# Projections in 64-row halves: the matmuls of q, k, v and the output as pairs in two phases, in a new order

## The chip, the cores and the metric

The kernel runs on one core of a Trainium2 chip. What counts is the time of one launch on the device, in microseconds (us): 454.13, the median of three runs from 454.07 to 455.19. The engines are TensorE (PE in the rows; PEld is its loading of weights), VectorE (DVE), ScalarE (ACT), GpSimd (POOL) and SyncE (SP), whose queue issues all the DMAs.

## What is computed

Eight batches of 8 heads, 576 positions, head size 64. Two attentions are added, and a mixture of four causal attention experts, two of which are chosen for each position, follows. Cut to the core:

```
out_up    = repeat(softmax(q_d @ k_d.T / 8) @ v_d, 4)        # q_d, k_d, v_d: means of 4 positions
out_local = softmax(where(|i-j| < 4, q @ k.T / 8, -1e9)) @ v
x         = (out_up + out_local) as [8, 576, 512]
logits    = x @ w_gate                                       # two of four experts, softmax over the two
for e in range(4):
    a    = softmax(causal((x @ wq[e]) @ (x @ wk[e]).T / 8))
    out += weight_of(e) * (a @ (x @ wv[e]) @ wo[e])
```

## The kernel before

Stage 1 of a batch works on four pairs of heads: local scores (`s1_local`, tile `sc`, line L515), pooled scores (`s1_down`, tile `scd`, L588), their transposes (`tp`, L383) and their products with v (`s1_out`, tile `o`, L650 to L662), from which x comes (L670). x is split into a rounded part `xh` (L675) and a rest `xl` (L676), so that a product with a weight, which is split too, is three matmuls at the rate of rounded fp32: `xh` with the high and the low part of the weight, and `xl` with the high part.

Stage 2 makes the projections. `project` (L686) makes q or k of two experts, 128 rows by 576 columns in a two-bank PSUM tile `pj`: twelve matmuls of 128 rows on 320 columns and twelve on 256 (four pairs of heads times three, L693). `project_by_pair` (L708) is the same for the first q, in the order in which the x arrive. `s2_v` makes v and the gate's logits for 128 positions at a time (12 matmuls on 260 columns, L739, two position blocks in one PSUM tile `pv`), and for the last 64 positions (8 matmuls, L748).

Stage 3 makes the causal scores (`sq`, L852), their softmax (DVE L872, ACT L875, and L883 on POOL or DVE), the transposes of its rows (`tq`, L383), the products with v (tile `o`, L966 and L970) and the output projection (`po`, L989: six matmuls on 256 and six on 320 columns; L1011 for the last batch).

So TensorE works in three shapes, which the rows show as rows * columns of the weights: 128*128 (`pj`, `pv`, `po`), 64*128 (the transposes `tp` and `tq`, in twos on the upper and the lower 64 rows) and 64*64 (`sc`, `scd`, `sq`, `o`, four at a time in the quarters of the array).

All PSUM use goes through four tiles of two banks (`big`). The order in which every step is issued is a table of numbers, `SEQ`, an entry for each step with the engine that does it; -1 is a filler matmul on zeros (`wu`, L472) that keeps TensorE busy. Work of stage 1 of a batch, stage 2 of the one before and stage 3 of the one before that stands mixed in it. A step's `alloc` names the tiles that it takes over and whose earlier readers it waits for.

Of the kernel before, what the change touches and what calls it, by code (L numbers as in the profile page):

```python
# [29 lines left out]
    968, 1092, 1040, 1044, 892, 1168, 100, 112, 104, 1332, 1336, 836, 1233, 1049, 972, 980, 1508, 828, 824, 820,  # L30
    1069, 1212, 1216, 1220, 1052, 1340, 1056, 1224, 1228, 976, 1152, 1156, 728, 732, 1172, 1008, 1012, 1513, 984,
    988, 1436, 934, 1098, 1160, 992, 1108, 1112, 1100, 1104, 1245, 1248, 1548, 1552, 1556, 1560, 1252, 1256, 1261,
    1432, 1753, 1564, 1004, 1460, 1464, 1568, 1572, 1468, 1756, 1576, 1264, 1268, 1580, 1164, 1272, 1277, 1292,
    1344, 1180, 1520, 1524, 1116, 1120, 1124, 1496, 1472, 1476, 1528, 1532, 1348, 1352, 1128, 1132, 1136, 1480,
    1537, 1540, 1356, 1544, 1484, 1488, 1384, 1284, 1500, 1296, 1288, 1300, 1176, 1184, 1360, 1364, 1368, 1592,
    1388, 1504, 1584, 1144, 1492, 1588, 1648, 1644, 2073, 1241, 1141, 1596, 1608, 1612, 1600, 1604, 1304, 1308,
    1312, 1316, 1616, 1392, 1396, 1765, 1768, 1320, 1716, 1328, 1324, 1620, 1624, 1720, 1728, 1016, 1020, 1400,
    1404, 1408, 2077, 1773, 1776, 1724, 1780, 1784, 1672, 1676, 1412, 1416, 1516, 1790, 1372, 1376, 1820, 2128,
    1680, 1732, 1736, 1740, 1744, 1420, 1424, 1280, 1429, 117, 1380, 1824, 2132, 1828, 1832, 2016, 1708, 1629, 1792,
    1712, 1796, 2085, 1664, 1668, 1444, 2328, 1188, 1192, 1836, 1685, 1688, 1448, 1440, 1652, 1660, 1988, 1656,  # L40
    1992, 2324, 2020, 2088, 1840, 1844, 2092, 1692, 2024, 1848, 2096, 1696, 1700, 1749, 2100, 1852, 2532, 2536,
    2028, 2032, 1760, 1996, 2004, 2000, 2409, 1856, 2116, 2248, 2252, 2413, 2104, 2540, 1632, 1636, 1640, 1704,
    2080, 2120, 2124, 2036, 2040, 2044, 2048, 1861, 1864, 1916, 1921, 1800, 1804, 1808, 2940, 1812, 1868, 1880,
    1884, 1872, 1876, 1924, 1936, 2352, 2356, 1928, 1932, 1888, 1944, 1892, 1948, 1940, 1904, 1908, 1912, 1897,
    1972, 1976, 109, 1901, 2108, 2944, 2464, 2360, 1980, 1984, 2472, 2476, 1953, 1956, 1816, 1968, 1960, 1965, 2365,
    2368, 2468, 2876, 2880, 2884, 2052, 2056, 2372, 2888, 2060, 2064, 2377, 2380, 2384, 2288, 2300, 2304, 2168,
    2180, 2172, 1452, 1456, 2136, 2140, 2144, 2332, 2292, 2184, 2176, 2296, 2212, 2340, 2848, 2336, 2984, 2980,
    2008, 2012, 2852, 2068, 2948, 2992, 2996, 2988, 2148, 2152, 2892, 2156, 2188, 2192, 2200, 2196, 2224, 2216,
    2421, 2424, 2428, 2432, 2165, 2896, 2436, 2440, 2308, 2900, 2160, 2572, 2576, 2580, 2228, 2220, 2284, 2396,
    2400, 2404, 2600, 2604, 2204, 2208, 2444, 2608, 2312, 2316, 3433, 2544, 2548, 2232, 2236, 2240, 2612, 2552,  # L50
    2556, 3008, 3012, 2320, 3016, 3020, 2480, 2484, 2488, 2492, 2496, 2904, 2500, 2508, 2417, 2344, 2348, 2864,
    2505, 2616, 2620, 2664, 2668, 2672, 2256, 2456, 2260, 2624, 2628, 2460, 2448, 2452, 2632, 2244, 2388, 2856,
    2392, 3436, 2908, 2636, 2644, 2640, 2560, 2564, 2708, 2720, 2724, 2728, 2264, 2268, 2712, 2768, 2780, 2784,
    2772, 2776, 2272, 2276, 2280, 2732, 3360, 3364, 3368, 2512, 2516, 2520, 2789, 2792, 2716, 3044, 2736, 3048,
    3272, 2953, 2956, 2960, 3372, 2868, 2860, 3100, 2568, 3660, 3340, 3332, 3348, 3344, 2872, 2740, 2744, 2752,
    2796, 3056, 3376, 3380, 3024, 3028, 3093, 3032, 3036, 2524, 3052, 2749, 3385, 2964, 2969, 3624, 3628, 3276,
    3316, 3480, 3040, 2529, 3388, 3392, 3320, 3060, 3588, 3592, 3632, 3720, 3097, 2972, 2978, 3065, 3068, 3073,
    3724, 3728, 3732, 3736, 2800, 2584, 2756, 2588, 3656, 3596, 3336, 2760, 2765, 2592, 2596, 3740, 3744, 2648,
    2652, 2657, 2804, 2808, 3196, 3200, 3188, 3193, 2912, 3236, 2916, 3241, 3076, 3504, 3508, 3244, 3248, 3105,
    3108, 3113, 3684, 3688, 2812, 2816, 3760, 3764, 3445, 4052, 3116, 2820, 2824, 2828, 3448, 3692, 3696, 2832,  # L60
    3120, 3204, 3208, 3212, 3216, 4049, 2836, 3972, 2660, 3000, 3976, 3004, 2676, 2680, 2685, 3453, 3456, 3460,
    3124, 2844, 2840, 3464, 3220, 3700, 3704, 3709, 3712, 3130, 3470, 3224, 3228, 3716, 3769, 3232, 3080, 2692,
    3084, 3088, 2696, 2700, 3816, 3820, 3824, 3829, 3132, 3136, 3512, 2688, 3517, 3988, 3980, 2704, 3984, 3140,
    3160, 3144, 3152, 3520, 3524, 3528, 3532, 3536, 3164, 3156, 3148, 3440, 3540, 3544, 3548, 2920, 2924, 3280,
    3284, 3292, 3296, 3396, 3400, 3404, 3168, 4000, 3408, 4004, 3172, 3180, 3288, 3412, 3301, 3176, 4008, 4012,
# [12 lines left out]
    4656, 4660, 4380, 4384, 3864, 3868, 3872, 4468, 4836, 4844, 3876, 4940, 4944, 4948, 4952, 4332, 4336, 4344,
    4600, 4604, 4608, 3956, 3960, 3965, 4340, 4348, 4352, 4956, 4356, 4361, 4368, 3892, 4960, 5516, 4440, 5692,
# [1051 lines left out]
```

## Time and profile before

| | |
|---|---|
| median of the runs | 454.13 us |
| span of the profiled execution (first to last instruction) | 451.9 us; the 2.2 us to the median lie outside the span |
| PE busy | 441.2 us, 98% of the span |
| DVE, ACT, POOL busy | 362.5, 346.1, 301.2 us (80, 77, 67%) |
| the chain that ended last | PE for 87% of it |
| clock that TensorE was granted | 0.996 of 2.4 GHz |

A busy PE says little here, since matmuls overlap in the pipeline: what a matmul costs is the time from its start to the start of the next, and this is how the rows below are read.

### The profile page before, as it was taken

How to read it: one execution, taken by the hardware profiler on the slowest of the kernel's cores; microseconds unless marked ns; L12 is line 12 of the kernel's file. 1: busy time of each engine (PE TensorE's matmuls, PEld its weight loads, DVE VectorE, ACT ScalarE, POOL GpSimd, SP SyncE). 2: the span in 40 equal slices, each digit the busy share in tenths (PEclk: the TensorE clock that was granted, in tenths of full speed). 3: DMA queues.
4: the chain of work that ended last, by engine and by line, in shares of the span. 5: the costliest groups of instructions: out<-in, count | busy, mean ns of one | idle time of the engine just before them, and what ended most of it. 6: DMA issues, size and time to landing. Idle time of an engine off the chain costs nothing.

```text
span 451.9 us, 20317 instructions
## 1 busy us (share of the span) xinstructions
PE 441.2 (98%) x8374; PEld 401.8 (89%) x8375; DVE 362.5 (80%) x1020; ACT 346.1 (77%) x1099; POOL 301.2 (67%) x485
## 2 busy tenths in 40 slices
PE   8998999999999999999999999999999999999997
PEld 4787999989999889998899898999999999998876
DVE  8997989896859999777988999895897768445782
ACT  7985899687968898756867888775997687456783
POOL 6997878768867888665764776765984863304320
PEclk9998999999999999999999999999999999999999
DMA  8966537433344544543334432443272200200113
GB/s 251 281 191 188 169 99 212 123 112 83 89 141 137 155 126 136 158 141 89 113 108 160 118 99 65 133 140 92 62 220 63 70 1 4 80 28 14 52 57 106
DMA packets 44300, 52.70 MB, mean 117 GB/s; under 512 B 4144, under 2 KB 27184, under 8 KB 44208
## 3 DMA queue, kind: packets, MB, share of 16 engines
q1 hardware_dynamic: 44208, 51.40, 38.1%
q8 instruction: 66, 1.08, 1.0%
q14 instruction: 26, 0.21, 0.1%
HBM read 40.90 MB, written 9.44 MB: 111 GB/s over the span
## 4 chain that ended last, share of the span: by engine, by line
PE 87%; DVE 4%; DMA 4%; issue 2%; SPq 1%; ACT 1%; DVEq 0%; ACTq 0%
PE pj L693 20%; PE pv L739 10%; PE po L989 10%; PE sq L852 9%; PE o L966 8%; PE tq L383 6%; PE tp L383 5%; PE sc L515 4%; PE o L650 4%; PE scd L588 3%; DMA lv<-in_v_dram 3%; PE pv L748 2%; PE o L657 2%; PE po L1011 1%; PE o L970 1%
## 5 line engine op out<-in xcount | busy, mean ns | idle before, releaser
L875 ACT ACTIVATE pr<-pr,pst 128x384 f32<-128x384 f32 (+8 forms) x144 | 80.0, 558 | 13.3 <-DVE pst L872 12.6
L883 POOL TENSOR_SCALAR pr<-pr,pst,gt 128x64 f32<-128x64 f32 (+8 forms) x97 | 65.9, 687 | 16.2 <-DVE pst L880 12.0
L693 PE MATMUL pj<-xh,wqk_h 128*128 128x320 f32 (+1 forms) x248 | 74.8, 302 | 0.0
L693 PE MATMUL pj<-xh,wqk_l 128*128 128x320 f32 (+1 forms) x248 | 72.8, 293 | 0.0
L693 PE MATMUL pj<-xl,wqk_h 128*128 128x320 f32 (+1 forms) x248 | 72.7, 293 | 0.0
L872 DVE CUSTOM_DVE_ANT_0 pr<-sq,causal_t 128x384 f32<-128x384 f32 (+8 forms) x144 | 63.8, 484 | 5.2 <-PE sq L852 4.7
L852 PE MATMUL sq<-k,q 64*64 64x256 f32 (+6 forms) x768 | 52.2, 370 | 0.0
L693 PEld LDWEIGHTS pj<-xh,wqk_h 128*128 128x128 f32 x248 | 46.5, 188 | 2.5 <-issue 0.6
L693 PEld LDWEIGHTS pj<-xh,wqk_l 128*128 128x128 f32 x248 | 46.5, 188 | 0.0
L693 PEld LDWEIGHTS pj<-xl,wqk_h 128*128 128x128 f32 x248 | 46.5, 187 | 0.0
L978 POOL TENSOR_TENSOR ol<-oc,oh 128x256 fp32r<-128x256 f32 (+1 forms) x27 | 22.1, 822 | 32.4 <-ACT oh L977 22.6
L852 PEld LDWEIGHTS sq<-k,q 64*64 64x64 f32 x768 | 32.9, 133 | 7.0 <-issue 0.3
L598 ACT ACTIVATE dp<-scd,dst 128x144 f32<-128x144 f32 x96 | 35.2, 376 | 3.4 <-DVE dst L593 2.7
L739 PE MATMUL pv<-wvg_h,xh 128*128 128x260 f32 x128 | 37.0, 289 | 0.0
L739 PE MATMUL pv<-wvg_l,xh 128*128 128x260 f32 x128 | 36.1, 282 | 0.0
L739 PE MATMUL pv<-wvg_h,xl 128*128 128x260 f32 x128 | 36.1, 282 | 0.0
L676 POOL TENSOR_TENSOR xl<-x,xh 128x576 fp32r<-128x576 f32 x22 | 32.4, 1473 | 4.5 <-ACT xh L675 4.0
L536 POOL TENSOR_TENSOR lp<-lp,lst 128x640 f32<-128x640 f32 x24 | 31.9, 1336 | 4.4 <-DVE lst L535 3.7
L383 PE MATMUL tq<-ident,pr 64*128 64x64 f32 x736 | 33.2, 228 | 1.4 <-DVE pst L872 0.6
L989 PE MATMUL po<-oh,wo_h 128*128 128x256 f32 (+1 forms) x112 | 34.0, 304 | 0.0
L989 PE MATMUL po<-oh,wo_l 128*128 128x256 f32 (+1 forms) x112 | 33.0, 294 | 0.0
L383 PEld LDWEIGHTS tq<-ident,pr 64*128 64x128 f32 x736 | 27.1, 138 | 6.5 <-issue 2.6
(182 smaller groups left out, 1438.8 us busy)
## 6 DMA issues: line engine op xcount, KB each, us to landing
lv<-in_v_dram SPq DMA_DIRECT2D x64, 160.0 KB, 3.7
lq<-in_qT_dram SPq DMA_DIRECT2D x32, 292.0 KB, 3.5
lk<-in_kT_dram SPq DMA_DIRECT2D x32, 292.0 KB, 3.9
out_dram<-ot SPq DMA_DIRECT2D x28, 288.0 KB, 2.3
lr<-in_v_dram SPq DMA_DIRECT2D x28, 256.0 KB, 3.2
lr<-in_v_dram SPq DMA_DIRECT2D x56, 32.0 KB, 3.0
wst<-in_wqk_dram SPq DMA_DIRECT2D x1, 1024.0 KB, 9.1
vx<-vg SPq DMA_DIRECT2D x8, 128.0 KB, 2.6
```

Source lines behind the costliest of these rows:

```text
L383: T.transpose(ps()[:, 512 * x + z[x]:512 * x + z[x] + 64], data[r, 0:128], ident[r, r])
L536: op("l_nrm", "GV", (pool_tt(n), dve(n)), lambda e: eng[e].tensor_tensor(p(), p(), st[:, :, 2:3].to_broadcast([128, NT, W]), op=OP.mult), ...
L598: A.activation(p()[:, t, :], scs()[:, at * t:at * t + SD], AF.Exp, bias=st[:, t, 4:5], scale=1.0 / 128.0, accum_out=st[:, t, 0:1])
L676: op("xl", "GV", (1360, dve(576)), lambda e: eng[e].tensor_tensor(xl(), x(), xh()[:, 0:S].bitcast(F32), op=OP.subtract), r=[x, (xh, 0)], w ...
L693: T.matmul(ps()[:, H0 + n0:H0 + n1], ww[:, c, w0 + 128 * p:w0 + 128 * p + 128], xx[b, c]()[:, n0:n1], start=(i == 0), stop=(i == 3 * NP - 1))
L739: T.matmul(ps()[:, at:at + 260], xx[b, c]()[:, 128 * t:128 * t + 128], ww[:, c, :], start=(i == 0), stop=(i == 3 * NP - 1))
L852: T.matmul(pss[x][0]()[halves[e ^ turned(t)], at_of[x] + at + to:at_of[x] + at + to + n1 - n0], q()[r, 64 * t:64 * t + 64], k()[r, n0:n1], ...
L872: op("s_max", "V", dve(n) + 4, lambda x=x, t=t, n=n, src=src: V.tensor_tensor_reduce(rows_of[t], src(), causal_t[:, S - 64:S + 256] if t = ...
L875: op("s_exp", "A", 281 + n / 1.2, lambda x=x, t=t, n=n: A.activation(rows_of[t], rows_of[t], AF.Exp, bias=st[:, x, 4:5], scale=-1.0, accum ...
L883: op("s_nrm", "GV", (327 + n / 1.2 + max(0, n - 384) * 1.1, 189 + n / 1.92), lambda g, x=x, t=t, n=n: eng[g].tensor_scalar(rows_of[t], row ...
L966: T.matmul(obs[x]()[r, q0:q1], vg()[kr, j, 64 * (2 * p + e):64 * (2 * p + e) + 64], pt()[kr, e, j, q0:q1], start=j == 0, stop=j == len(job ...
L989: T.matmul(ps()[:, H1 + n0:H1 + n1], ww[:, p, 128 * c:128 * c + 128], xx[b, p]()[:, n0:n1], start=(i == 0), stop=(i == 5))
```

## The change

Each projection is cut into two 64-row halves. A matmul of 128 rows becomes a pair: one on the upper 64 rows, one on the lower 64, which write different halves of the output (288 columns each, in the two banks of one PSUM tile). That is phase 0; in phase 1 the two swap halves, so that each half of the output gets both halves of the rows. Phase 1 may not begin before both last matmuls of phase 0 have ended, for which there is a semaphore `done`. The two phases are steps of their own, and other work may stand between them.

```diff
-    def project(kind, b, p, w0, alloc):
-        ps = big("pj")
-        def mm(n0, n1):
-            i = 0
-            for c in range(NP):
-                for ww, xx in ((wqk_h, XH), (wqk_l, XH), (wqk_h, XL)):
-                    T.matmul(ps()[:, H0 + n0:H0 + n1], ww[:, c, w0 + 128 * p:w0 + 128 * p + 128],
-                             xx[b, c]()[:, n0:n1], start=(i == 0), stop=(i == 3 * NP - 1))
-                    i += 1
...
+    done, passed = tc.alloc_semaphore("done"), [0]
+    HP = 512 - S // 2
+    class Chain:
...
+        def part(self, phase, cs, final):
+            for c in cs:
+                for i in range(3):
+                    for h, r in enumerate(halves):
+                        if phase == 1 and c == 0 and i == 0 and h == 0:
+                            T.wait_ge(done, self.at)
+                        z = h ^ phase
+                        mine = T.matmul(self.out(z), self.w(c, i, z)[r], self.m(c, i, z)[r], start=phase == 0 and c == 0 and i == 0,
+                                        stop=phase == 1 and c == self.n - 1 and i == 2)
+                        if phase == 0 and c == self.n - 1 and i == 2:
+                            mine.then_inc(done, 1)
...
+    def chain(kind, cost, ps, out, w, m, n, reads, split):
...
+        for phase in range(2):
+            for x, cs in enumerate(split[phase]):
+                op(kind, "T", cost * len(cs), lambda phase=phase, cs=cs: ch.part(phase, cs, cs[-1] == n - 1),
+                   r=[y for c in cs for y in reads(c)], w=[ps], alloc=[] if phase or x else [ps])
+    SPLIT = {False: (((0, 1), (2, 3)),) * 2, True: (((0,), (1,), (2,), (3,)), ((0, 1), (2, 3)))}
```

q and k, v (two position blocks at once) and the output projection of all batches but the last go through `chain`. The last 64 positions of v are made in pairs without phases: upper and lower rows go into two banks, and two more steps, a copy (`v_t0`, ACT) and an add (`v_t1`, DVE), bring them together:

```diff
+                for i, ww in enumerate((wvg_h, wvg_l)):
+                    for x, r in enumerate(halves):
+                        T.matmul(ps()[:, 512 * x:512 * x + 260], XH[b, c]()[r, S - 64:S + 64], ww[r, c, :],
+                                 start=(c == 0 and i == 0), stop=(c == NP - 1 and i == 1))
+        op("v_t0", "A", act(260), lambda: A.copy(vt(), ps()[:, 0:260]), r=[ps], w=[vt], alloc=[vt])
+        op("v_t1", "V", dve(260), lambda: V.tensor_tensor(vt(), ps()[:, 512:772], vt(), op=OP.add), r=[ps], w=[vt])
```

Everywhere, the SBUF tile that a result is copied to is now taken over by the copy and no longer by the matmuls ahead of it, as here:

```diff
-        op("local", "T", 630, mm, r=[q, k], w=[sc], alloc=[sc, p])
+        op("local", "T", 630, mm, r=[q, k], w=[sc], alloc=[sc])
```

And the whole table is new:

```diff
 SEQ = (
-    0, 173, 2112, 4, 177, 24, 136, 140, 189, -1, 192, 197, 120, 268, -1, 124, 232, -1, -1, -1, -1, -1, 200, 20,
...
```

What that does to the order is seen at two places. PE, the middle of the run: before, the end of a q projection (`pj`) with the transposes behind it and the v projection (`pv`) that follows.

```order
L693 MATMUL pj<-xh,wqk_h 128x256
L693 MATMUL pj<-xh,wqk_l 128x256
L693 MATMUL pj<-xl,wqk_h 128x256
L383 MATMUL tp<-ident,dp 128x64 [waits DVE_49]
L383 MATMUL tp<-ident,dp 128x64 x9
L383 MATMUL tq<-ident,pr_131 128x64 [waits DVE_49,Pool_49]
L383 MATMUL tq<-ident,pr_131 128x64 x3
...
L383 MATMUL tp<-ident,lp 128x64 [waits DVE_49]
L383 MATMUL tp<-ident,lp 128x64 x9
L739 MATMUL pv<-wvg_h,xh 128x260 [waits Activation_49]
```

After the change, a q or k projection in the middle of the run: the products with v ahead of it, the end of phase 0, what stands between, and the start of phase 1.

```order
L957 MATMUL o_5411<-ptb,vg 64x64 x4
L694 MATMUL pj<-xh,wqk_h 128x288 [waits DVE_49,PE_49]
L694 MATMUL pj<-xh,wqk_h 128x288
...
L694 MATMUL pj<-xl,wqk_h 128x288 x2
L374 MATMUL tp<-ident,lp 128x64 [waits DVE_49,Pool_49]
L374 MATMUL tp<-ident,lp 128x64 x9
L374 MATMUL tq<-ident,pr_127 128x64 [waits DVE_49,Pool_49]
L374 MATMUL tq<-ident,pr_127 128x64 x3
L374 MATMUL tq<-ident,pr_132 128x64 x4
L694 MATMUL pj<-xh,wqk_h 128x288 [waits done]
L694 MATMUL pj<-xh,wqk_h 128x288
```

A projection, which was one block of 24 matmuls, is now two of 24, and transposes stand between them and behind them. SP, the start: before, the weights of q and k (`wst<-in_wqk_dram`) are the 13th transfer, ahead of the two `lr` transfers that wait for POOL's memset of their tile.

```order
L455 DMA wst<-in_wqk_dram 128x4x512 [waits DMAHW5_49]
L488 DMA lq<-in_qT_dram 128x584 [waits DMAHW6_49,DVE_49,PE_49]
L489 DMA lk<-in_kT_dram 128x584 [waits DMAHW7_49,DVE_49]
L496 DMA lr_96<-in_v_dram 16x512 [waits DMAHW0_49,Pool_49]
L496 DMA lr_95<-in_v_dram 16x512 [waits DMAHW1_49,Pool_49]
L499 DMA lv<-in_v_dram 64x5x128 [waits DMAHW2_49]
```

After the change they stand behind two of them, and the weights of v (`wst<-in_wvg_dram`) behind the v of the first two pairs of heads.

```order
L446 DMA wst<-in_wvg_dram 128x4x260 [waits DMAHW4_49]
L479 DMA lq<-in_qT_dram 128x584 [waits DMAHW5_49,DVE_49,PE_49]
L480 DMA lk<-in_kT_dram 128x584 [waits DMAHW6_49,DVE_49]
L487 DMA lr_96<-in_v_dram 16x512 [waits DMAHW7_49,Pool_49]
L487 DMA lr_96<-in_v_dram 16x512 [waits DMAHW0_49]
L446 DMA wst<-in_wqk_dram 128x4x512 [waits DMAHW1_49]
```

That memset is the 38th row on POOL, where the two before were its 27th and 37th.

## Rows read from the trace of the kernel before

**Rows 1.** The page, parts 1 and 4: busy time, and the chain that ended last.

```profile
PE 441.2 (98%) x8374; PEld 401.8 (89%) x8375; DVE 362.5 (80%) x1020; ACT 346.1 (77%) x1099; POOL 301.2 (67%) x485
...
PE 87%; DVE 4%; DMA 4%; issue 2%; SPq 1%; ACT 1%; DVEq 0%; ACTq 0%
```

**Rows 2.** What PE waited for: us in total, times, longest.

```profile
PE sc L515 <- issue: 1.7, 1, 1.7
...
PE tp L383 <- issue: 1.1, 1, 1.1
PE sc L515 <- DVE oc L975: 0.8, 1, 0.8
...
PE tq L383 <- ACT ptb L325: 0.3, 1, 0.3
```

**Rows 3.** Timeline of PE and PEld, 199.9 to 204.7: start, duration, what.

```profile
199.94 0.31 PE L693 MATMUL pj<-xh,wqk_h 128*128 128x320 f32 x1
...
201.70 0.28 PE L693 MATMUL pj<-xh,wqk_h 128*128 128x256 f32 x1
...
202.99 0.28 PE L693 MATMUL pj<-xl,wqk_h 128*128 128x256 f32 x1
203.20 0.52 PE L383 MATMUL tp<-ident,dp 64*128 64x64 f32 x10
203.56 0.35 PE L383 MATMUL tq<-ident,pr 64*128 64x64 f32 x6
203.75 0.47 PE L383 MATMUL tp<-ident,lp 64*128 64x64 f32 x10
204.16 0.39 PE L739 MATMUL pv<-wvg_h,xh 128*128 128x260 f32 x1
204.38 0.28 PE L739 MATMUL pv<-wvg_l,xh 128*128 128x260 f32 x1
```

**Rows 4.** Timeline of PE and PEld, 244.2 to 245.4.

```profile
244.18 0.74 PEld L515 LDWEIGHTS sc<-lk,lq 64*64 64x64 f32 x40
...
244.98 0.19 PEld L693 LDWEIGHTS pj<-xh,wqk_h 128*128 128x128 f32 x1
244.98 0.41 PE L693 MATMUL pj<-xh,wqk_h 128*128 128x320 f32 x1
245.09 0.19 PEld L693 LDWEIGHTS pj<-xh,wqk_l 128*128 128x128 f32 x1
245.24 0.30 PE L693 MATMUL pj<-xh,wqk_l 128*128 128x320 f32 x1
```

**Rows 5.** Timeline of PE, 295.1 to 295.6.

```profile
295.11 0.47 PE L383 MATMUL tq<-ident,pr 64*128 64x64 f32 x8
295.51 0.59 PE L588 MATMUL scd<-kd,qd 64*64 64x144 f32 x10
```

**Rows 6.** Timeline of PE at 20.05 and at 222.07: plain fp32, two records a matmul.

```profile
20.05 1.72 PE L573 MATMUL pv<-lv,pool 128*128 128x128 f32 x14
...
222.07 1.94 PE L966 MATMUL o<-ptb,vg 64*64 64x320 f32 x31
```

**Rows 7.** Timeline of PE at 6: a wait of PE for its own matmuls.

```profile
6.29 0.38 PE L472 MATMUL wu<-zero 128*128 128x512 bf16 x1 [0.16 <-PE scd L588]
```

**Rows 8.** Busy time from 38 to 45 (PE, PEld, DVE, ACT, POOL; clock, DMA, GB/s).

```profile
38.00:45.00 7.00, 7.00 (x149) 6.65 (x146) 5.40 (x11) 2.30 (x7) 4.38 (x6) 0.76 0.68 193
```

**Rows 9.** The start: timelines of SP, POOL, ACT and DVE, and a DMA's landing.

```profile
9.76 0.38 SPq L455 DMA_DIRECT2D wst<-in_wqk_dram  x1
...
wst<-in_wqk_dram SPq DMA_DIRECT2D x1, 1024.0 KB, 9.1
...
13.87 0.52 POOL L436 MEMSET lr<- 128x512 f32 x1
...
32.83 0.62 ACT L459 CAST wqk_h<-wst 128x512 fp32r<-128x512 f32 x1
...
39.63 0.74 DVE L670 SCALAR_TENSOR_TENSOR x<-up,o 128x576 f32<-128x576 f32 x1
```

More of the change, by code (lines that the diff above doesn't have):

```diff
@@ L680, in s1_out @@
            r=[x, (xh, 0)], w=[(xh, 1)])
[L683 removed]
+    H0 = 192
     QS, KS, VG, VX, GT, OH, OL = {}, {}, {}, {}, {}, {}, {}
[L686 to L699 removed]
@@ L701, in project_by_pair @@
-    def project_by_pair(kind, b, p, w0, alloc):
-        ps = big("pj")
-        def mm(c):
-            for n0, n1 in ((0, 320), (320, S)):
-                for i, (ww, xx) in enumerate(((wqk_h, XH), (wqk_l, XH), (wqk_h, XL))):
-                    T.matmul(ps()[:, H0 + n0:H0 + n1], ww[:, c, w0 + 128 * p:w0 + 128 * p + 128], xx[b, c]()[:, n0:n1],
-                             start=(c == 0 and i == 0), stop=(c == NP - 1 and i == 2))
-        for c in range(NP):
-            op(kind, "T", dense(3, 320) + dense(3, 256), lambda c=c: mm(c), r=[(XH[b, c], 0), XL[b, c]] + needs(wqk_h)[c:c + 1],
-               w=[ps], alloc=[] if c else [ps] + alloc)
-        return ps
@@ L715, in s2_q, with __init__ @@
-    def s2_q(b, p, kind="q", w0=0, to=QS, bufs=NQ):
-        x = to[b, p] = buf(wk, [128, S], kind, bufs)
-        ps = (project_by_pair if (kind, b, p) in PAIRWISE else project)(kind, b, p, w0, [x])
-        op(kind + "_ev", "AV", (act(576), dve(576)), lambda e: copy(e, x(), ps()[:, H0:H0 + S]), r=[ps], w=[x])
+    done, passed = tc.alloc_semaphore("done"), [0]
+    HP = 512 - S // 2
+    class Chain:
+        def __init__(self, ps, out, w, m, n, group):
+            self.ps, self.out, self.w, self.m, self.n, self.group, self.at = ps, out, w, m, n, group, 0
+        def part(self, phase, cs, final):
[9 more added lines that the diff above has]
+                            mine.then_inc(done, 1)
+                            tc.no_tile_sem_insts.add(mine.ins.name)
+                            tc.add_to_no_dep_group(self.group, mine.ins)
+            if phase == 0 and final:
+                passed[0] += 2
+                self.at = passed[0]
+            if phase == 1 and final:
+                tc.declare_fence(mine.ins, group=self.group)
@@ new lines, in s2_q @@
+    def s2_q(b, p, kind="q", w0=0, to=QS, bufs=NQ):
+        x, ps = buf(wk, [128, S], kind, bufs), big("pj")
+        to[b, p] = x
+        three = ((wqk_h, XH), (wqk_l, XH), (wqk_h, XL))
+        chain(kind, 396, ps, lambda z: ps()[:, HP + S // 2 * z:HP + S // 2 * (z + 1)],
+              lambda c, i, z: three[i][0][:, c, w0 + 128 * p:w0 + 128 * p + 128],
+              lambda c, i, z: three[i][1][b, c]()[:, S // 2 * z:S // 2 * (z + 1)], NP,
+              lambda c: [(XH[b, c], 0), XL[b, c]] + needs(wqk_h)[c:c + 1], SPLIT[b == 0])
+        op(kind + "_ev", "AV", (act(576), dve(576)), lambda e: copy(e, x(), ps()[:, HP:HP + S]), r=[ps], w=[x], alloc=[x])
@@ L918, in s2_trans @@
             need = sorted(set(y for t, j in js for y in ((t, t - 2) if j == "d" and t < 8 else (t,))))
-            o = op("trans", "T", 2 * QT * len(js) + 35, tr, r=[PR[t] for t in need], w=[ps], alloc=[ps] + first)
-            for part in parts:
-                if PT[b, p, part] not in first:
-                    o.deps.add(PT[b, p, part].owner)
+            op("trans", "T", 2 * QT * len(js) + 35, tr, r=[PR[t] for t in need], w=[ps], alloc=[ps])
             runs = []
@@ L943, in s2_trans @@
             op("t_ev", "AV", (act(k) + m, dve(k) + m), lambda e, ev=ev: ev(e), r=[ps],
-               w=[(PT[b, p, x[0]], (x[0], x[2], x[3], x[6])) for x in runs])
+               w=[(PT[b, p, x[0]], (x[0], x[2], x[3], x[6])) for x in runs], alloc=first)
     def s2_av(b, p, qlo, qhi):
@@ L995, in s2_out @@
-        op("wo_ev", "AV", (act(576), dve(576)), lambda e: copy(e, ot(), ps()[:, H1:H1 + S]), r=[ps], w=[ot])
+        three = ((wo_h, OH), (wo_l, OH), (wo_h, OL))
+        chain("wo", 397, ps, lambda z: ps()[:, HP + S // 2 * z:HP + S // 2 * (z + 1)],
+              lambda p, i, z: three[i][0][:, p, 128 * c:128 * c + 128],
+              lambda p, i, z: three[i][1][b, p]()[:, S // 2 * z:S // 2 * (z + 1)], 2,
+              lambda p: [(x[b, p], n0) for x in (OH, OL) for n0 in (0, CUT)] + needs(wo_h), (((0, 1),),) * 2)
@@ L1034, in stage2 @@
             if p == 0:
-                for t in range(5):
-                    yield "v", 1.42 if t < 4 else 0.95, s2_v, (b, t)
+                for t in (0, 2):
+                    yield "v", 2.85, s2_v, (b, t)
+                yield "tail", 0.95, s2_tail, (b,)
                 yield "gate", 0.01, s2_gate, (b,)
```

118 lines of the change are left out of this document (40 added, 78 removed), and 281 rows, old and new, of the table SEQ.

## The prediction

> **What bounds the kernel now.** I read the page's busy shares first. PE is busy for 98% of the span, DVE for 80%, ACT for 77%, POOL for 67%; the chain that ended last runs on PE for 87% of its length [rows 1]. So PE's own work sets the time, unless PE waits. The list of PE's waits says how much it does: two "issue" gaps of 1.7 and 1.1 us, both in the first 38 us, and after 45 us only four waits for other engines, from 0.8 to 0.3 us and 2.2 us together, a mean of 0.54 [rows 2]. The last place where PE loses something is from 38 to 45 us, where it was granted 0.76 of the 2.4 GHz clock: 7 x 0.24 = 1.7 us [rows 8]. What is left to win or lose is therefore what PE pays for each matmul and for each change between its shapes, and this is read from the timeline, start to start.
>
> **The matmuls themselves.** On 320 columns a projection's twelve matmuls start over 199.94 to 201.70, 0.1467 each; on 256, eleven over 201.70 to 202.99, 0.1173 each [rows 3]. That is 0.46 ns a column, so 288 columns cost 0.132. A projection was 12 x (0.1467 + 0.1173) = 3.17 us; now it is 24 pairs on 288 columns. If a pair costs what one full matmul of its columns costs, that is 24 x 0.132 = 3.17, and nothing changes. Whether it does, no row shows for this shape. The two halves must load their weights at once and stream at once. For the loading: forty loads of 64 columns took 0.74 us, 0.0185 each, while a load of 128 columns exposes 0.11 (244.98 to 245.09) [rows 4]; even if a 64-column load needs only half of that, 0.055 (an estimate), three are under way together, so both row halves load at once. For the streaming: 31 quarter-matmuls of plain fp32, 1,024 columns for each quarter in all, lasted 1.94 us, 1.9 ns a column, and seven full matmuls of 128 columns 1.72, also 1.9 [rows 6]; so row halves lose nothing by working side by side. I take 0.132 for the pair. The bounds: one column a clock at 2.4 GHz, 288/2.4 = 0.120, and the dearest full matmul of a projection, 0.1467 [rows 3]. There are 32 x 24 = 768 pairs for q and k, 16 x 24 = 384 for v and 28 x 12 = 336 for the output: 1,488. So the term is **0**, with ends at -17.9 us (-0.012 each) and +21.9 (+0.0147 each). It is by far the most sensitive one: 3 ns a pair make 4.5 us.
>
> The Trainium skill's "TensorE: Matmul & The Clock Gate", section on LDWEIGHTS, speaks against the change: a load takes its columns divided by 1.2 in ns, whatever its rows, so a half of 64 rows costs as much as a full load, 107 ns; the 0.11 exposed agrees. If the two loads of a pair queued up, each pair would cost some 0.21 by that page; the forty loads in 0.74 speak against it.
>
> **Changes of shape.** PE drains when its shape changes. From `pj` to the transposes 0.21 us pass (202.99 to 203.20) instead of 0.12; from the transposes to `pv` five pairs of transposes take 0.41 (203.75 to 204.16), where three take 0.19 without a change (0.063 a pair), so 0.31 would be due [rows 3]. That is 0.09 for a change. With it the first weights are exposed: after a change to 128*128 the second matmul starts 0.22 after the first (204.16 to 204.38) instead of 0.12, and 0.26 (244.98 to 245.24) instead of 0.147 [rows 3, 4], so 0.11; after a change to transposes five pairs take 0.36 (203.20 to 203.56) instead of 0.31 [rows 3], so 0.05. Transposes to 64*64 agree: four pairs take 0.40 instead of 0.25 [rows 5]. A change into 128*128 thus costs 0.20, any other 0.14.
>
> I counted the changes in PE's order from the first projection on. Before: 44 into 128*128 (15 from transposes, 29 from 64*64) at 0.20 = 8.8; 33 from 128*128 to transposes, 11 from it to 64*64, 35 from transposes to 64*64 and 17 back, 96 at 0.14 = 13.4; together 22.2 us. After, the projections have the transposes' shape, 64*128. So 46 steps from transposes to a pair cost only the exposed load that a transpose does not already pay, 0.11 - 0.06 = 0.05, that is 2.3; 62 steps from pairs to transposes cost nothing; 31 from 64*64 to pairs at 0.20 = 6.2; 15 from pairs to 64*64, 34 from transposes to 64*64 and 18 back, 67 at 0.14 = 9.4; together 17.9. The term is **-4.3 us**.
>
> The page "TensorEngine Tiling (Array Packing)" of the Trainium skill, section Key Properties, has the same rule: a change of the mode drains the array, another tile of one mode does not. The 0.09 agrees; that transposes and pairs share a mode no row here shows, and this is the first rival of loss below.
>
> **The wait between the phases.** Phase 1 waits until the last pair of phase 0 has ended. A matmul lasts 0.31 from start to end [rows 3], and PE waiting for its own results resumed 0.16 after their end [rows 7]; the next start was due after 0.13 anyway. So 0.34 us of other work must lie between. Of 76 waits, one has nothing (the first q, in the start), one has three pairs of transposes (0.19) and four have five (0.31); the rest have over 0.4. Uncovered: 0.34 + 0.15 + 4 x 0.03 = **+0.6 us**; the price is 0.34 for each further wait whose cover goes, at most 26 us.
>
> **The start.** SP's q and k weights were issued at 9.76 and took 9.1 to land; now they stand behind an `lr` transfer that waits for POOL's 38th row, about where the 37th stood, the memset at 13.87 [rows 9]. Issued near 15, they land near 24, ahead of the last cast at 32.83 [rows 9]: hidden, or up to 2 us if ACT's casts bunch. The last x of batch 0 was made at 39.63 as DVE's row 81 [rows 9]; now it is row 74. Seven rows at 5.40/11 = 0.49 [rows 8] are 3.4 us less work ahead of it, but PE has some 3.2 us less done by then, so most of that is only exchanged. The fillers fall from 24 to 5; they cost nothing where PE waited anyway. The two gaps and the slow clock are 1.1 + 1.7 + 1.7 = 4.5 us, of which some goes: **-1.0**, ends -4.4 and +2.
>
> **At nothing.** The copy and the add of `v_tail`, eight times some 0.7 us on ACT and DVE, lie in those engines' idle 20%. Taking over an SBUF tile later frees no PE time, since PE's waits after 45 us are not for such tiles; if the cover goes, each new PE wait costs 0.54 [rows 2]. The last batch's output keeps its matmuls.
>
> **The sum.** -4.3 + 0.6 - 1.0 + 0 = -4.7 us. The profiled span of 451.9 becomes 447.2; with the 2.2 us outside it, 449.4, against the median of 454.13.
>
> **The rivals.**
> - Pairs quicker than full matmuls. 0.126, half way to a column a clock, gives -8.9: 440.5; the bound gives 431.5. For it: two halves can hide each other's gaps. Against: 0.46 ns a column leaves little to hide. Chance 0.14.
> - The gain is eaten, 452.8 to 455.5: four PSUM tiles are now held through two phases with other work between, so evictions and the next user come later. Seven to twelve more waits of 0.54 do it. Against: PE hardly waits now. This is also the case in which the shapes' price was hidden and the change does not do what it says. Chance 0.14.
> - Slower, by one mechanism: transposes and pairs do not share a mode. Then 46 steps cost 0.20 instead of 0.05 (+6.9) and 62 cost 0.14 instead of 0 (+8.7): 449.4 + 15.6 = 465.0. It decides from 0.056 us for each of these 108 steps (6.1 us up to 455.5). Against: the rows name both 64*128, and in 64*64 other tiles follow without a pause. Chance 0.07.
> - Slower, as pairs cost 8 ns more (two loads and two matmuls to issue for one): +11.9, 461.3; from 4.1 ns on it is slower. Or the PSUM waits are over 12. Chance 0.13.
> - The two loads in series: 2 x 0.11 = 0.22 for a pair instead of 0.132, 0.088 x 1,488 = +131 us: 580. Chance 0.02.
>
> **How the numbers follow.** My forecast, 446 to 452.7, has 0.50; 449.4 is its time. A measurement here tells 0.3%, 1.4 us, from no change. Faster is the forecast and the quicker pairs, with a little of their edges, 0.65; the same 0.14; slower 0.21. The range goes down to 442 (pairs at 0.127) and up to 459 (pairs 6 ns dearer, or half the steps at full price), which leaves about one in ten out on either side.
>
> **What would show it.** In the profile after: pairs of 288 columns at 0.132 from start to start, 24 in 3.17 us; from the last transpose to the first pair no drain, so five transposes ahead of it at 0.31; PE waits on `done` below 1 us in all; PE still 98% busy, with waits after 45 us near 2 us; the span near 447. It is wrong if pairs are off by 3 ns or more, if the steps between transposes and pairs cost like changes, or if PE's list of waits names PSUM tiles' readers many times.

## The result, and the profile after the change

The changed kernel takes 460.19 us (median of 20 runs), the kernel before 453.94 in the same comparison: ratio 1.0108, 95% interval 1.0082 to 1.0134. Four of the changed kernel's 20 runs were in a slower state and are left out of the ratio; the other 16 have a median of 458.9. By the ratio it is slower by 4.9 us, where 4.7 us less were forecast. The profiled execution has a span of 457.3 us, 5.4 more than before.

The page's busy shares and its chain, which answer to [rows 1]:

```profile
PE 439.4 (96%) x9908; PEld 404.7 (88%) x9908; DVE 371.5 (81%) x1031; ACT 341.0 (75%) x1091; POOL 303.9 (66%) x487
...
PE 71%; DVE 9%; POOL 7%; ACT 5%; DMA 4%; issue 3%; SPq 0%; POOLq 0%; DVEq 0%; ACTq 0%
```

PE is busy for 1.8 us less, and its share of the chain that ended last fell from 87% to 71%: DVE, POOL and ACT now take 21% of it, where they took 5%. So PE waits. The list of its waits (us in total, times, longest), which answers to [rows 2]:

```profile
PE tp L374 <- DVE pd L318: 1.6, 1, 1.6
...
PE sc L506 <- ACT ot L316: 1.0, 1, 1.0
...
PE pj L694 <- POOL xl L667: 0.8, 1, 0.8
PE tq L374 <- DVE pt L318: 0.6, 1, 0.6
```

Busy time in two stretches of the middle (PE, PEld, DVE, ACT, POOL; clock, DMA share, GB/s), the first two lines before the change, the last two after it:

```profile
45.00:200.00 155.00, 154.94 (x3080) 144.49 (x3078) 133.54 (x373) 128.65 (x412) 120.14 (x184) 1.00 0.45 131
200.00:400.00 200.00, 198.56 (x3687) 184.92 (x3688) 159.05 (x455) 147.23 (x469) 128.04 (x202) 1.00 0.31 96
...
45.00:200.00 155.00, 153.34 (x3723) 144.82 (x3719) 140.25 (x377) 121.75 (x391) 122.94 (x186) 1.00 0.47 130
200.00:400.00 200.00, 195.19 (x4453) 182.27 (x4445) 161.63 (x462) 147.21 (x479) 129.86 (x207) 1.00 0.35 101
```

PE is idle for 0.06 and 1.44 us there before the change, and for 1.66 and 4.81 after it. The clock is the same.

A projection and its neighbours in the timeline of PE, which answers to [rows 3]; x2 is a pair:

```profile
205.80 0.28 PE L694 MATMUL pv<-wvg_h,xh 64*128 64x260 f32 x2
205.91 0.29 PE L694 MATMUL pv<-wvg_l,xh 64*128 64x260 f32 x2
...
206.40 0.28 PE L694 MATMUL pv<-wvg_h,xl 64*128 64x260 f32 x2
206.52 0.47 PE L374 MATMUL tp<-ident,lp 64*128 64x64 f32 x10
206.83 0.47 PE L374 MATMUL tp<-ident,dp 64*128 64x64 f32 x10
207.11 0.37 PE L694 MATMUL pv<-wvg_h,xh 64*128 64x260 f32 x2
207.31 0.28 PE L694 MATMUL pv<-wvg_l,xh 64*128 64x260 f32 x2
```

Five pairs from 205.80 to 206.40 are 0.12 each, as one full matmul of 260 columns was. From the last pair to the transposes 0.12 pass as well: no drain. Back again nothing is lost at the step either (five pairs of transposes in 0.28, where five in a row cost 0.31), but the first pair takes 0.20 instead of 0.12. Together the step back costs 0.05.

**Where the 5.4 us are.** I added up, over all of PE's records, the time from each start to the next beyond what the record's columns are worth (0.46 ns a column for the projections, and so on), and sorted it by what stood at the place. "Stall" is a place where the next start comes over 70 ns later than columns, shape and first load explain; it holds a wait's visible idle time and the late starts around it.

| | before | after | difference |
|---|---|---|---|
| lost up to 45 us | 20.3 | 20.5 | +0.3 |
| stalls after 45 us | 3.1 (9 places) | 10.2 (28 places) | +7.1 |
| shapes and first loads after 45 us | 24.3 | 22.2 | -2.1 |
| rest | 3.2 | 3.4 | +0.2 |
| sum, to the end of the last matmul | 50.9 | 56.3 | +5.4 |

The sorting is good to some 0.5 us, as a stall beside a change of shape falls partly into either row.

So by this sorting the shapes gave less than forecast, and the stalls, forecast at nothing but 0.6 us for the phases, took 7.1. The idle time that the profile shows of PE after 45 us goes the same way: 2.3 us before, 6.9 after.

### The profile page after: what moved, and what is told of

It is laid out like the page before. It is cut to its first block, busy times and chain, and to the rows that moved or that the text cites. A ratio compares the mean times of both kernels' runs of the same rounds, so it can differ in the third digit from the quotient of the medians.

```text
span 457.3 us, 23412 instructions
## 1 busy us (share of the span) xinstructions
PE 439.4 (96%) x9908; PEld 404.7 (88%) x9908; DVE 371.5 (81%) x1031; ACT 341.0 (75%) x1091; POOL 303.9 (66%) x487
## 4 chain that ended last, share of the span: by engine, by line
PE 71%; DVE 9%; POOL 7%; ACT 5%; DMA 4%; issue 3%; SPq 0%; POOLq 0%; DVEq 0%; ACTq 0%
PE pj L694 18%; PE sq L843 7%; PE o L953 7%; PE pv L694 7%; PE po L694 6%; PE tq L374 4%; PE sc L506 4%; PE o L641 4%; PE tp L374 3%; PE scd L579 2%; PE o L648 2%; PE po L992 2%; DVE pr L874 1%; PE pv L564 1%; POOL pr L874 1%
## 5 line engine op out<-in xcount | busy, mean ns | idle before, releaser
L866 ACT ACTIVATE pr<-pr,pst 128x256 f32<-128x256 f32 (+8 forms) x144 | 80.0, 557 | 15.0 <-DVE pst L863 14.7
L694 PE MATMUL pj<-xh,wqk_h 64*128 64x288 f32 x512 | 82.0, 309 | 0.1
L694 PE MATMUL pj<-xl,wqk_h 64*128 64x288 f32 x512 | 77.7, 292 | 0.8 <-POOL xl L667 0.8
L694 PE MATMUL pj<-xh,wqk_l 64*128 64x288 f32 x512 | 77.4, 291 | 0.0
L874 POOL TENSOR_SCALAR pr<-pr,pst,gt 128x256 f32<-128x256 f32 (+8 forms) x89 | 58.5, 665 | 26.2 <-DVE pst L871 10.0
L863 DVE CUSTOM_DVE_ANT_0 pr<-sq,causal_t 128x576 f32<-128x576 f32 (+8 forms) x144 | 64.7, 484 | 8.3 <-PE sq L843 7.7
L694 PEld LDWEIGHTS pj<-xh,wqk_h 64*128 64x128 f32 x512 | 50.1, 185 | 2.6 <-issue 1.0
L694 PEld LDWEIGHTS pj<-xl,wqk_h 64*128 64x128 f32 x512 | 50.0, 184 | 1.2 <-POOL xl L667 1.0
L694 PEld LDWEIGHTS pj<-xh,wqk_l 64*128 64x128 f32 x512 | 50.0, 185 | 0.0
L694 PE MATMUL pv<-wvg_h,xh 64*128 64x260 f32 x256 | 39.1, 292 | 0.0
```

What stands on the lines that cost most here:

```text
L694: mine = T.matmul(self.out(z), self.w(c, i, z)[r], self.m(c, i, z)[r], start=phase == 0 and c == 0 and i == 0, stop=phase == 1 and c == se ...
L863: op("s_max", "V", dve(n) + 4, lambda x=x, t=t, n=n, src=src: V.tensor_tensor_reduce(rows_of[t], src(), causal_t[:, S - 64:S + 256] if t = ...
L866: op("s_exp", "A", 281 + n / 1.2, lambda x=x, t=t, n=n: A.activation(rows_of[t], rows_of[t], AF.Exp, bias=st[:, x, 4:5], scale=-1.0, accum ...
L874: op("s_nrm", "GV", (327 + n / 1.2 + max(0, n - 384) * 1.1, 189 + n / 1.92), lambda g, x=x, t=t, n=n: eng[g].tensor_scalar(rows_of[t], row ...
```

## The experiments

Theory W: PE now waits for inputs that come late, and this outweighs what the shapes give. Its first rivals: S, the shapes give nothing; I, PE starves on twice the instructions; J, the waits of one profile are chance. Later W was split into W1 (it is the loads that land late) and W2 (it is the order of the other engines). The ratios are to the kernel before, on the same chip.

**The changed kernel again (e1).** No edit.

> The changed kernel as it is, for a second profile beside the others. Theory W (waits: PE now waits for late transfers and late evictions, 6.7 us of visible idle time after 45 us against 2.2 before, and this outweighs what the shapes give): idle time of PE after 45 us again 5 to 9 us, mostly at the same places (198.9, 245.2, 322.4, 340.5 in the first profile), ratio to before 1.008 to 1.013. Rival J (jitter: the waits of that one profile are chance): other places, and a sum that may lie anywhere from 2 to 9 us.

Measured: 1.0154 (1.0111 to 1.0198), span 457.4; stalls after 45 us 9.0 us at 29 places, the loss up to 45 us 21.6. All eleven stalls over 0.3 us of the first profile are there again at the same steps (`pd` 1.2, `xl` 0.9, `pt` 0.7), two of them shorter than 0.3. The order makes them; J is out. The ratio is a little above what was expected.

**Full rows in the new order (e2).**

```diff
+            z = phase
             for c in cs:
                 for i in range(3):
-                    for h, r in enumerate(halves):
-                        if phase == 1 and c == 0 and i == 0 and h == 0:
-                            T.wait_ge(done, self.at)
-                        z = h ^ phase
-                        mine = T.matmul(self.out(z), self.w(c, i, z)[r], self.m(c, i, z)[r], start=phase == 0 and c == 0 and i == 0,
...
+                    T.matmul(self.out(z), self.w(c, i, z), self.m(c, i, z), start=c == 0 and i == 0,
+                             stop=c == self.n - 1 and i == 2)
```

> The changed kernel with every pair replaced by one matmul of 128 rows on the same columns (phase 0 makes the first half of the output, phase 1 the second), no wait between the phases; order and tiles are the same. Theory W: pairs cost what full matmuls cost, but the shape changes come back: some 49 steps from transposes to a projection at 0.23 instead of 0.09 and some 65 back at 0.11 instead of 0.03 is about +12 us, less 1 for the waits between phases: ratio to before about 1.035 (1.025 to 1.045). Theory S (transposes and pairs share nothing, the shapes' term of the prediction was never there): same time as the changed kernel, 1.011. Theory I (PE starves on twice the instructions): faster than the changed kernel by the 2 to 4 us of its issue gaps, ratio 1.00 to 1.007.

Measured: 1.0385 (1.0338 to 1.0432), by the ratios 10.5 us over e1. Its timeline of PE at a projection's two sides:

```profile
221.49 0.29 PE L691 MATMUL pj<-xl,wqk_h 128*128 128x288 f32 x1
221.71 0.52 PE L374 MATMUL tp<-ident,lp 64*128 64x64 f32 x10
222.06 0.41 PE L374 MATMUL tq<-ident,pr 64*128 64x64 f32 x8
222.40 0.40 PE L691 MATMUL pj<-xh,wqk_h 128*128 128x288 f32 x1
222.64 0.30 PE L691 MATMUL pj<-xh,wqk_l 128*128 128x288 f32 x1
222.77 0.29 PE L691 MATMUL pj<-xl,wqk_h 128*128 128x288 f32 x1
```

The step to transposes takes 0.22 instead of 0.13, and back four pairs take 0.34 instead of 0.25 and the first matmul 0.24 instead of 0.13. In this order pairs are worth 10 to 14 us against full rows, and the steps between transposes and projections are enough to account for it: S is out. I is out as the main cause, since with half the projections' instructions the time is longer. Its visible idle time after 45 us is 5.1 us, where the changed kernel has 6.9 and in e1 5.8, so a us or two for I is not excluded (its stalls add up to 10.6 us, but in this run PE stood at a granted clock of 0.50, which is 1.2 GHz, from 256.8 to 260.2, behind a wait of 2.2 us). The run also says what the new order costs: with full matmuls the old order takes 454 us and the new one 472, and transposes stand next to projections 108 times in it, where it was 48.

**The tiles taken over as before (e3).** The lists of tiles given back to TensorE's steps, as here:

```diff
-        op("local", "T", 630, mm, r=[q, k], w=[sc], alloc=[sc])
+        op("local", "T", 630, mm, r=[q, k], w=[sc], alloc=[sc, p])
```

> The changed kernel with the SBUF tiles taken over by TensorE's steps again, as before the change; order and pairs stay. If the move of the tiles is worth nothing, as predicted: ratio as the changed kernel's, 1.011. If it gains something that the prediction missed: slower, 1.015 to 1.03, with new waits of PE for readers of SBUF tiles (ot, pt, pd, oc). If taking over later is what blocks ACT and DVE (as ot does at 240.9, where ACT's copy waits for a store to land and PE waits for ACT): faster by 1 to 2 us, 1.007.

Measured: 1.0122 (1.0081 to 1.0163), stalls 10.2. The instructions of all five engines turned out to stand in the same order as in the changed kernel: with a written table these lists matter for PSUM tiles alone. So this is one more run of the same program, and that part of the change is nothing by itself.

**The stores on ACT's queue (e4), and a third ot buffer with it (e5); the same in the kernel before (e10).**

```diff
-NQ, NK, NOT = 3, 2, 2
+NQ, NK, NOT = 3, 2, 3
...
-        op("st", "D", 1150, lambda: nc.sync.dma_start(out[b, 128 * c:128 * c + 128, :], ot()), r=[ot])
+        op("st", "D", 1150, lambda: nc.scalar.dma_start(out[b, 128 * c:128 * c + 128, :], ot()), r=[ot])
```

> The changed kernel with the 28 stores of the output issued by ACT instead of SP. SP waits some 110 us in all at these stores, with the loads queued behind them. Theory W, if the loads are late because they stand behind stores: PE's idle time after 45 us falls from 6.7 to 2 to 4 us, time 2 to 5 us less than the changed kernel's (ratio to before 1.000 to 1.006). If loads are late for their buffers, not for the stores: no change or slower, as ACT has 28 issues more (1.010 to 1.016).

> The stores issued by ACT as in the run before, and a third buffer for ot, the tile that they store. In the run before, the waits at 322 and 340 were gone but a new one of 2.86 us had come at 247, where ACT's copy into ot waited for a store to land. Theory W (late inputs, each wait another one): that wait goes too, PE's idle time after 45 us falls to 2 to 4 us, and the time to 2 to 4 us below the changed kernel's: ratio to before 1.002 to 1.008. Rival (the waits are only moved: what one releases, the next engine holds up): idle time stays at 5 to 7 us, ratio 1.010 to 1.016.

> The kernel before with the stores issued by ACT and three ot buffers, and nothing else. If that helps only where PE waits for late inputs (2.2 us in the kernel before): 0.997 to 1.003. If it is a gain of its own, in any order, it is as large here as in the changed kernel: 0.992 to 0.996, and then it says nothing on the change.

Measured: e4 1.0116 (1.0060 to 1.0172), stalls 11.6; e5 1.0060 (1.0023 to 1.0097), e10 1.0029 (1.0004 to 1.0053). In e4 the waits at 322 and 340 are gone, and 2.86 us for `ot` came instead, as e5's expectation tells; the time is not in the range that W gave if loads were late behind stores (1.000 to 1.006). e5 is perhaps a little faster than the changed kernel, but its profile has stalls of 11.1 us, with 2.0 for `xl` at 339, so what it gains isn't seen there: inconclusive. It is no gain of its own, as the kernel before has none from it.

**POOL relieved (e6).** The scaling of the local weights on 2 of 10 blocks only:

```diff
-            p(), p(), st[:, :, 2:3].to_broadcast([128, NT, W]), op=OP.mult), r=[ST], w=[p])
+            p()[:, 0:2], p()[:, 0:2], st[:, 0:2, 2:3].to_broadcast([128, 2, W]), op=OP.mult), r=[ST], w=[p])
```

> The changed kernel with the last scaling of the local weights (L527) done on 128 of the 640 columns only, so that POOL has some 26 us less to do (28 instructions of 1.29 us, now near 0.35) and DVE a little less; the local attention's weights stay unscaled elsewhere. Theory W with POOL as the late engine (xl at 340, dp, lp and pr come from it): PE's idle time after 45 us falls by 2 to 4 us, ratio to before 1.002 to 1.008. If PE waits for transfers and evictions, and not for POOL: no change, 1.010 to 1.016.

Measured: 1.0143 (1.0095 to 1.0190), stalls 11.9; POOL is busy for 277.6 us instead of 303.9, and the waits for `xl` and `pd` are 1.6 us each. POOL's work is not what is late. What POOL waits for is told by the chain that ended last, in the changed kernel's first profile (start, duration, what):

```profile
332.86 4.30 DMA lr<-in_v_dram
...
337.33 1.28 POOL lr L558
...
338.69 0.73 POOL vd L559
339.43 1.83 POOL xl L667
341.25 0.04 issue
341.30 0.40 PE pj L694 x2
```

An `lr` that landed at 337.2 held up POOL, behind it stood `xl`, and PE waited for that. The queue that issued this `lr` (timeline of SP in the same profile):

```profile
313.40 0.54 SPq L480 DMA_DIRECT2D lk<-in_kT_dram  x1
314.05 0.61 SPq L490 DMA_DIRECT2D lv<-in_v_dram  x1
314.70 0.65 SPq L484 DMA_DIRECT2D lr<-in_v_dram  x1
315.41 13.68 SPq L490 DMA_DIRECT2D lv<-in_v_dram  x2
329.20 1.64 SPq L487 DMA_DIRECT2D lr<-in_v_dram  x1
...
332.86 0.42 SPq L487 DMA_DIRECT2D lr<-in_v_dram  x1
```

SP stood from 316.6 to 328.5 at the second of these two `lv`, whose buffer was not free, and nine transfers then went out within 6 us. The `lk` of 313.40 belongs to an earlier crowd of this kind, thirteen transfers from 307.3 to 315.4; it took 5.05 us to land, and by the chain the wait for `pd` at 322 goes back to it.

**The old order with pairs for q and k (e7).** In the kernel before, `project`'s two steps become the two phases:

```diff
-        op(kind, "T", dense(12, 320) + 70, lambda: mm(0, 320), r=xs, w=[ps], alloc=[ps] + alloc)
-        op(kind, "T", dense(12, 256) + 10, lambda: mm(320, S), r=xs, w=[ps])
+        op(kind, "T", dense(12, 320) + 70, lambda: ch.part(0, range(NP), True), r=xs, w=[ps], alloc=[ps] + alloc)
+        op(kind, "T", dense(12, 256) + 10, lambda: ch.part(1, range(NP), True), r=xs, w=[ps])
```

> The kernel before with one part of the change: its q and k projections (31 of 32) as pairs in two phases, in the old order, v and the output as they were. In that order 21 of the 31 have their two steps side by side, so the wait between phases is uncovered. By the prediction's prices: 7 steps from transposes 0.14 cheaper and 19 to transposes 0.11 cheaper (-3.1 us), 31 new changes between the 128-row projections and pairs at 0.2 (+6.2), 21 waits of 0.2 to 0.34 (+4.4 to +7.1): 7 to 10 us slower than before, ratio 1.016 to 1.023. If the shape of the pairs is not what a change costs, the first two terms are gone and it is 1.010 to 1.016; if pairs were slower than full matmuls by themselves, over 1.03.

Measured: 1.0244 (1.0191 to 1.0298), 11.1 us, a little more than expected. The border of two phases in PE's timeline:

```profile
210.63 0.31 PE L701 MATMUL pj<-xh,wqk_l 64*128 64x288 f32 x2
210.76 0.31 PE L701 MATMUL pj<-xl,wqk_h 64*128 64x288 f32 x2
211.14 0.40 PE L701 MATMUL pj<-xh,wqk_h 64*128 64x288 f32 x2
211.38 0.30 PE L701 MATMUL pj<-xh,wqk_l 64*128 64x288 f32 x2
211.51 0.30 PE L701 MATMUL pj<-xl,wqk_h 64*128 64x288 f32 x2
```

0.38 instead of 0.13, and 0.24 for the first pair behind it: some 0.34 for an uncovered wait (0.32 to 0.35 over all 21 places). In the old order these waits alone take some 7 of the 11 us, so the phases need an order that puts something between them.

**The lr loads early (e8), and with the stores on ACT (e9).** 61 entries of the table moved, each `lr` load right behind the step that frees its buffer.

> The changed kernel with 61 of the lr transfers (from batch 1 on) issued earlier in SP's queue: each right behind the step that frees its buffer, instead of some 30 to 190 steps later, behind other loads and stores. All other engines keep their order. In the profiles of the changed kernel the wait of PE for xl at 340 goes back to an lr that landed at 337 and held POOL up. Theory W: that wait goes and POOL is held less; PE's idle time after 45 us 1 to 3 us less than the 5.5 to 6.7 of the changed kernel, time 1 to 3 us less, ratio to before 1.005 to 1.010. Rival (the waits are only moved on, or SP is blocked elsewhere): ratio 1.010 to 1.016.

> The same on top of the stores issued by ACT and three ot buffers (which came to 1.006). Theory W: both gains add, PE's idle time after 45 us under 4 us, ratio 1.000 to 1.005. Rival: no gain over 1.006, as something else then comes last.

Measured: e8 1.0798 (1.0758 to 1.0838), e9 1.0817 (1.0764 to 1.0871), stalls 33 and 35 us. PE's waits in e8:

```profile
PE o L635 <- DMA lv<-in_v_dram: 10.8, 6, 3.0
PE tq L368 <- DVE pr L868: 5.8, 1, 5.8
PE sc L500 <- ACT ot L310: 4.1, 1, 4.1
```

A miss for the expectation of W: SP now stood over 100 us in all at the early `lr`, for POOL to free their buffers, and `lv` came late instead. That transfers decide over PE is clear from it: nothing but 61 places in SP's queue has changed (and one small DVE instruction, which stands four places later), and 31 us were lost. Not all of it is waiting. PE waited 5.8 us up to 212.3, and at 211.4 its granted clock fell to 0.50, which is 1.2 GHz:

```profile
211.50:218.20 6.70, 5.90 (x116) 5.50 (x120) 4.76 (x12) 0.56 (x1) 2.51 (x3) 0.50 0.28 67
```

There are four such stretches in e8 after 45 us, each at a wait of 2.5 to 5.8 us and 17 us together, and none in the changed kernel. At half the clock they cost PE some 8 us (an estimate).

**No loads from batch 2 on (e11), the same in the kernel before (e12), and a third lv buffer (e13).** e11 and e12:

```diff
+        if b >= 2:
+            q, k, vw = LQ[1, 2 + c % 2], LK[1, 2 + c % 2], LV[1, 2 + c % 2]
...
+        start = nc.sync.dma_start if b < 2 else lambda *a: None
```

with `start` for the loads' `nc.sync.dma_start`. e13:

```diff
-            vw = buf(ld, [128, 5, 128], "lv", NLV)
+            vw = buf(ld, [128, 5, 128], "lv", 3)
...
-        cmt, gst = buf(wk, [128, 2, 5, 4, 4], "cm"), buf(wk, [128, 3, 5], "gs")
+        cmt, gst = buf(wk, [128, 2, 5, 4, 4], "cm", 1), buf(wk, [128, 3, 5], "gs")
```

> The changed kernel without the loads of q, k and v from batch 2 on (its stages go on with the tiles of batch 1, so the attention is that of other data; all compute instructions and the stores stay). Theory W1 (PE's stalls come from loads that land late, directly or through POOL and DVE which wait for them): PE's stalls after 45 us, 9 to 10 us with their restarts in the changed kernel, fall to 3 or 4, and the time by 5 us or more: ratio to before 1.000 or below. Theory W2 (they come from the other engines' order, the loads being late only with them): stalls stay at 7 to 10 us, ratio 1.006 to 1.013.

> The same for the kernel before, as the control: its stalls after 45 us are 3.1 us, only one or two of them behind a load. W1 and W2 both: little to win, 0.994 to 1.000. If it gains as much as the changed kernel does (over 4 us), loads cost something in general, by their traffic, and say nothing on the change.

> The changed kernel with a third buffer for lv (paid for with one of the two of the gate's small tile cm). Five blocks of products with v wait in their middle for the second lv transfer, 1.7 us together, and SP stands 26 us for lv's buffers with other loads behind. W1: stalls fall by 2 to 4 us, ratio 1.002 to 1.008. W2: 1.008 to 1.014.

Measured: e11 0.9989 (0.9964 to 1.0014), e12 1.0007 (0.9975 to 1.0038), e13 1.0128 (1.0089 to 1.0168). Stalls after 45 us are 4.5 us in e11, 3.8 in e12, 10.7 in e13. Two stretches of the middle in e11, and the longest of PE's waits, the first four of them in the start:

```profile
45.00:200.00 155.00, 153.91 (x3687) 145.40 (x3687) 140.26 (x379) 122.37 (x394) 124.06 (x186) 1.00 0.10 32
200.00:400.00 200.00, 198.93 (x4532) 185.69 (x4532) 163.28 (x466) 147.95 (x477) 128.45 (x205) 1.00 0.09 30
...
PE scd L582 <- DVE qd L545: 1.2, 1, 1.2
PE wu L351 <- DVE zero L348: 1.2, 1, 1.2
PE o L644 <- issue: 1.2, 1, 1.2
PE scd L582 <- DVE kd L547: 1.1, 1, 1.1
PE tq L374 <- DVE pt L318: 0.5, 1, 0.5
PE sq L846 <- ACT ot L316: 0.3, 1, 0.3
```

Without the loads the changed kernel loses its whole deficit, 1.2% of the time, and the kernel before gains nothing (it had few stalls to lose). PE's idle time in the two stretches is 1.09 and 1.07 us. The waits for `xl` and `lv`, and the long ones for `pd` and for `ot` at 245, are gone with the loads, while ACT, DVE and POOL keep their order. That is W1, as far as that the stalls need the loads. The profile of e11 is of the quickest of its twelve runs (451.03 us; median 453.81).

e13 is a miss for W1: its ratio is where W2 had it. One more buffer for `lv`, the load at which SP stood longest, gives nothing back. SP stops at the same place all the same, for 12.3 us up to 330.0, now at an `lr`. And the buffer is paid for with one of the gate's, so it is not a test of `lv` alone.

## Why the prediction was wrong, step by step

**Pairs: right.** 0.133 us from pair to pair on 288 columns after 45 us (median; 0.132 forecast), 0.120 on 260. e2 has the full matmul of 288 columns at 0.133. The rival of loads in series is out: each load of a half is recorded with 0.184 us, and the two of a pair fit into 0.133. The rule of the Trainium skill that a load costs by its columns whatever its rows ("TensorE: Matmul & The Clock Gate", LDWEIGHTS) is no hindrance here, as the halves load at once: one behind the other, they would take more than 0.133 by the 0.11 that the prediction reads for an exposed load.

**Transposes and pairs share their shape: right.** The drain between them is nil, as above, and e2 shows it back at 0.09 a step. This agrees with the Trainium skill's rule in "TensorEngine Tiling (Array Packing)", Key Properties, that the array drains when the mode changes and not when only the tile does. The sharpest rival, 465.0, is refuted.

**The size of that term: right at the steps, short in the sum.** -4.3 was forecast; the sorting has -2.1. The steps themselves are as forecast, in number (46 and 62) and in price. Where PE does not wait, I took the time over a step, from two or three pairs ahead of it to two or three behind, less what these pairs cost in a row. From transposes to a pair it is 0.05 us (median), and 0.20 from transposes to a full matmul in the kernel before; back again it is nothing (-0.01), where it was 0.14. That makes 15 x 0.20 + 33 x 0.14 = 7.6 us before and some 2 us after, as the prediction has it; the steps to and from 64*64 cost about the same in both kernels. So the 2.2 us that the sorting lacks are lost somewhere else, and no run places them. One hint: from the first projection on, the blocks of 64*64 matmuls last 137.2 us in e11 and 135.4 in the kernel before, with 0.7 and 0.8 us of visible idle time in them.

**The wait between the phases: right.** Forecast 0.34 uncovered; e7 has 0.34 in the mean. In the changed kernel one stands open at 42 us (0.49 to the next start, 0.24 behind it) and one at 429 (0.36 and 0.24), some 0.8 us together for the 0.6 forecast.

**The start: off by 1.3 to 2.3.** -1.0 was forecast; it lost 0.3 us in the first profile and 1.3 in e1 against the kernel before, inside the bounds that the prediction gave. The fillers' gain and the earlier x were given back by waits for `qd`, `kd` and, in e1, `lq` (3.7 us).

**"At nothing": the step that failed.** The prediction said that PE's waits after 45 us would stay at 2.2 us, and looked for new ones among the four PSUM tiles; the profile after has 6.9 us. The prediction followed the new table on PE, and on SP's queue only in the start, for the weights. On the same queue the table also moved some 200 loads and stores of the middle, and from there most of the 7.1 us of stalls come (e11 has 5.7 less). By the two waits that were followed back, at 322 and 340, it happens so: loads stand behind another transfer whose buffer isn't free, then go out in a crowd and land late (median 4.3 us for `lv` where it was 3.7, 4.1 for `lq` where it was 3.5, 3.7 for `lr` where it was 3.2), and hold up PE, or POOL and DVE and through them PE. That the stalls need the loads is shown by e11 against e12; that each of them comes about in this way is not shown. "The gain is eaten" had the right outline with the wrong resource, and a bound of twelve further waits, where the table has nineteen further stalls.

SP's own waits show what the new order did to the queue (two lines of before, then two of after: for `ot`'s copies and for `lv`'s buffers; us in total, times, longest):

```profile
SPq L996 <- ACT ot L325: 67.8, 15, 17.4
SPq L499 <- PE o L662: 47.0, 16, 7.0
...
SPq L977 <- ACT ot L316: 76.5, 9, 30.8
SPq L490 <- PE o L653: 26.4, 5, 11.6
```

Over all of them SP waits no longer than before, 314 us where it was 325, but less often and longer at a time. Between 45 and 400 us it stands still for over 8 us ten times, where it was twice, and from 45 us on ten or more transfers go out within 8 us ten times, where it was three. In e13 it stands still ten times too, and in e5 nine times. So it fits that no single change gave the loss back: each moves the places at which the queue stops and leaves their number.

**What stays open.** Which feature of the new queue makes the loads late is not settled: its stores ahead of loads (e4, e5), the `lv` buffers (e13) and the place of `lr` (e8) were each tried alone, and none gave it back beyond the doubt that e5 leaves. Nor is it settled whether the queue's own order is at fault or the engines that free the buffers late, as the queue waits for both. No version beat the kernel before; even without its loads the changed one only draws level with it, though the steps between shapes alone should have put it some 4 us ahead.

## What to carry to other kernels

An order that is written out moves every queue. Follow the DMA queue through the whole run, for each load what stands ahead of it and until when, with the same care as the engine that is the bound: where that engine is 98% busy, as here, a few late transfers outweighed a hundred cheaper changes of shape. And before a gain at the steps between two shapes is counted, count the steps that the new order adds: here pairs were worth 10 to 14 us, and the order that they needed cost more.

## What the runs showed of the hardware

Two 64-row matmuls on the two halves of the array take together what one of 128 rows takes on the same columns, 0.133 us on 288. Between transposes and such pairs, both 64*128, PE loses 0.05 us one way and nothing the other; between transposes and matmuls of 128 rows it is 0.20 and 0.14. A wait of PE costs more than the idle time that the profile shows: at 21 places of e7 the profile shows 0.06 to 0.09 us, while the next start is 0.24 us late and the pair behind it takes 0.10 more.
